# Output rows of a convolution and mixture kernel formed on TensorE, with a PSUM ring of three and two single banks

**Chip, cores, metric.** One core of one Trainium2 chip. The time is that of one execution on the device, in microseconds; the median of several executions is quoted with their spread. Engines are named as in the profile: PE (TensorE), PEld (its weight loads), DVE (VectorE), ACT (ScalarE), POOL (GpSimd), SP (SyncE).

## The reference

2048 tokens of 640 channels. A long convolution along the tokens makes the first residual; a router then picks 8 tokens for a gated feed-forward, whose result is added to those rows only. Cut to what the change touches:

```python
h = layernorm(x) * (1 + ca) + sa
x = x + ga * A(h, k, v, ...)             # conv by FFT, per channel
h = layernorm(x) * (1 + cb) + sb
# B: r = h @ w_r; idx = 8 largest r;  upd = h with  y(idx) added to 8 rows
x = x + gb * B(h, w_r, w_gate, w_up, w_down)
```

So each output row is x + gb * (layernorm(x) * (1 + cb) + sb), and 8 of the 2048 rows get a small addition afterwards.

## The kernel before

x lies in `xq`, 16 tiles of 128 tokens by 640. The steps run in a hand-written order; a star behind a step's name in that order puts its evacuation on DVE instead of ACT. Four PSUM tiles of two banks each serve everything:

```python
psum = ctx.enter_context(tc.tile_pool(name="psum", bufs=4, space=bass.MemoryType.PSUM))
```

The rows are made in three steps: the base x + gb*sb on PE (t_BS, and t_BL for the last 128 channels), the normalised row on ACT or DVE (t_N), and two DVE passes (t_F). The sums of squares for the layernorm run on ACT (t_S).

```python
    def t_BS():
        for j in range(8):
            # ... cut
            for i in range(2):
                nc.tensor.matmul(ps[:, i, :], lhsT=ident[:], rhs=gbs[:, 0:512], start=True, stop=False)
                nc.tensor.matmul(ps[:, i, :], lhsT=ident[:], rhs=xq[:, 2 * j + i, 0:512], start=False, stop=True)
            evac(h_["base", j // 4][:, 2 * j % 8:2 * j % 8 + 2, 0:512], ps[:])
            yield
    # ... cut
    def t_N():
        for m in range(M):
            if evac.vector:
                V.tensor_scalar(out=xn(m), in0=xq[:, m, :], scalar1=rs2[:, m:m + 1], scalar2=nm2[:, m:m + 1],
                                op0=ALU.mult, op1=ALU.add)
            else:
                nc.scalar.activation(out=xn(m), in_=xq[:, m, :], func=ACT.Identity, scale=rs2[:, m:m + 1],
                                     bias=nm2[:, m:m + 1])
            yield
    def t_F():
        for j in range(8):
            x2 = xq[:, 2 * j:2 * j + 2, :]
            V.tensor_tensor(out=x2, in0=xn(2 * j, 2).rearrange("p (m d) -> p m d", m=2),
                            in1=gbo[:, None, :].to_broadcast([P, 2, D]), op=ALU.mult)
            V.tensor_tensor(out=x2, in0=x2, in1=h_["base", j // 4][:, 2 * (j % 4):2 * (j % 4) + 2, :], op=ALU.add)
            # ... cut
```

## Time and profile before

| | |
|---|---|
| median of 3 runs | 186.74 us (184.03 to 187.41) |
| profiled span | 183.9 us, mean granted clock 0.919 |
| last attention block added | 147.0 |
| router score ready | 156.6 |
| last output row on DVE | 175.2 |
| small addition ready (delta) | 178.6 |

The lower four rows are landmarks, read from the order of time: the end of the instruction that writes the thing, counted from the start of the span. They cut the tail into stages. The chain of waits, followed back from the end, is spread over the engines:

```profile
DVE 27%; DMA 27%; PE 24%; ACT 12%; issue 6%; SPq 2%; POOLq 1%; POOL 0%; DVEq 0%; ACTq 0%
```

No engine holds the path alone. The totals, slices and windows stand in the prediction.

### The profile page before, as it was taken

How to read it: one execution, taken by the hardware profiler on the slowest of the kernel's cores; microseconds unless marked ns; L12 is line 12 of the kernel's file. 1: busy time of each engine (PE TensorE's matmuls, PEld its weight loads, DVE VectorE, ACT ScalarE, POOL GpSimd, SP SyncE). 2: the span in 40 equal slices, each digit the busy share in tenths (PEclk: the TensorE clock that was granted, in tenths of full speed). 3: DMA queues.
4: the chain of work that ended last, by engine and by line, in shares of the span. 5: the costliest groups of instructions: out<-in, count | busy, mean ns of one | idle time of the engine just before them, and what ended most of it. 6: DMA issues, size and time to landing. Idle time of an engine off the chain costs nothing.

```text
span 183.9 us, 4109 instructions
## 1 busy us (share of the span) xinstructions
PE 144.0 (78%) x1664; PEld 112.5 (61%) x1664; DVE 157.7 (86%) x283; ACT 136.2 (74%) x180; POOL 33.2 (18%) x81
## 2 busy tenths in 40 slices
PE   0669989985989999939999969999679578165850
PEld 0225979952768679837679759998577342024840
DVE  5869998988979899977599999989979996999930
ACT  4368789792897979775599979999448999996000
POOL 7997500005001022010010020020200102100003
PEclk9999999999999999995799999999999999955555
DMA  6999989999999999992041999994768099705540
GB/s 108 152 204 278 313 186 326 272 198 274 265 292 320 338 304 309 176 200 114 0 171 61 212 320 324 368 338 183 200 261 224 8 293 362 310 4 219 207 153 2
DMA packets 68668, 40.68 MB, mean 221 GB/s; under 512 B 44904, under 2 KB 64808, under 8 KB 68648
## 3 DMA queue, kind: packets, MB, share of 16 engines
q1 hardware_dynamic: 65160, 35.15, 72.7%
q0 software_dynamic: 1520, 5.25, 7.7%
q10 hardware_dynamic: 1968, 0.01, 0.7%
q8 instruction: 13, 0.21, 0.5%
q14 instruction: 7, 0.06, 0.1%
HBM read 24.67 MB, written 10.50 MB: 191 GB/s over the span
## 4 chain that ended last, share of the span: by engine, by line
DVE 27%; DMA 27%; PE 24%; ACT 12%; issue 6%; SPq 2%; POOLq 1%; POOL 0%; DVEq 0%; ACTq 0%
DMA kT<-in_A_k_dram 9%; PE ps L295 8%; ACT junk L404 7%; DMA kvd<-kvT 7%; DMA uA<-Ud 6%; DVE kvT L297 4%; DVE st L581 4%; PE ps L274 3%; PE ps L314 3%; DVE xq L641 3%; DMA Ud<-U 3%; DVE xq L643 3%; PE ps L384 2%; ACT U L58 2%; ACT A L58 2%
## 5 line engine op out<-in xcount | busy, mean ns | idle before, releaser
L58 ACT CAST A<-ps 128x1024 bf16<-128x1024 f32 x35 | 33.6, 1030 | 8.5 <-PE ps L274 8.5
L58 ACT CAST HX<-ps 128x1024 bf16<-128x1024 f32 x37 | 35.9, 1054 | 2.8 <-PE ps L318 2.8
L314 PE MATMUL ps<-A,FT 128*128 128x256 bf16 x160 | 36.2, 272 | 0.4 <-DVE kvT L297 0.4
L318 PE MATMUL ps<-A,FT 128*128 128x128 bf16 x160 | 35.0, 219 | 0.0
L316 PE MATMUL ps<-A,FT 128*128 128x128 bf16 x160 | 35.0, 219 | 0.0
L295 PE MATMUL ps<-kT,dg 128*128 128x512 bf16 x80 | 21.6, 426 | 7.0 <-DMA kT<-in_A_k_dram 7.0
L58 ACT CAST U<-ps 128x1024 bf16<-128x1024 f32 x20 | 19.8, 1048 | 5.0 <-PE ps L350 2.3
L295 PEld LDWEIGHTS <-dg 128*128 128x128 bf16 x80 | 8.5, 108 | 17.4 <-issue 3.8
L354 POOL DMA_DIRECT2D Ud<-U x10 | 5.7, 572 | 72.9 <-ACT U L58 62.9
L348 PE MATMUL ps<-IT,HX 128*128 128x256 bf16 x80 | 18.1, 273 | 0.8 <-DVE kvT L297 0.8
L350 PE MATMUL ps<-IT,HX 128*128 128x256 bf16 x80 | 18.1, 273 | 0.0
L297 DVE TENSOR_TENSOR kvT<-ps,vT 128x1024 bf16<-128x1024 f32 x10 | 12.1, 1220 | 6.9 <-PE ps L295 5.7
L318 PEld LDWEIGHTS <-FT 128*128 128x128 bf16 x160 | 15.7, 98 | 1.8
L316 PEld LDWEIGHTS <-FT 128*128 128x128 bf16 x160 | 15.6, 98 | 0.9 <-issue 0.8
L314 PEld LDWEIGHTS <-FT 128*128 128x128 bf16 x160 | 15.7, 98 | 0.3
L237 POOL TENSOR_SCALAR dg<-ident,shk_f 128x128 bf16<-128x128 bf16 x16 | 10.3, 659 | 20.0 <-PE ps L295 20.0
L384 PE MATMUL ps<-RAT,uA 128*128 128x128 bf16 x160 | 10.4, 219 | 4.2 <-DMA uA<-Ud 4.2
L404 ACT ACTIVATE junk<-xq 128x512 bf16<-128x512 bf16 (+1 forms) x23 | 12.2, 533 | 2.0 <-DVE xq L391 1.3
L389 DVE TENSOR_TENSOR t<-ps,h 128x1024 bf16<-128x1024 f32 x10 | 12.2, 1218 | 1.7 <-PE ps L384 1.6
L581 DVE BATCH_NORM_STATS2 st<-xq 128x6 f32<-128x320 bf16 x32 | 13.2, 478 | 0.5 <-DMA xq<-in_A_q_dram 0.5
L274 PE MATMUL ps<-RA,gA 128*128 128x256 bf16 x80 | 12.3, 309 | 1.5 <-DVE gA L281 1.5
L333 DVE TENSOR_TENSOR HX<-HX 128x2048 bf16<-128x2048 bf16 x10 | 12.2, 1225 | 0.4
(218 smaller groups left out, 308.6 us busy)
## 6 DMA issues: line engine op xcount, KB each, us to landing
Ud<-U POOLq DMA_DIRECT2D x10, 512.0 KB, 6.0
uA<-Ud SPq DMA_DIRECT2D x10, 512.0 KB, 6.5
early<-in_w_mod_dram SPq DMA_DIRECT2D x6, 800.0 KB, 7.3
gA<-in_A_ssm_k_dram SPq DMA_DIRECT2D x5, 512.0 KB, 5.0
kvd<-kvT SPq DMA_DIRECT2D x10, 256.0 KB, 3.9
xq<-in_A_q_dram SPq DMA_DIRECT2D x4, 640.0 KB, 6.4
xA<-kvd SPq DMA_DIRECT2D x5, 512.0 KB, 4.8
out_dram<-xq SPq DMA_DIRECT2D x4, 640.0 KB, 3.1
```

The source lines that it names most:

```text
L58: self.nc.scalar.copy(out=out, in_=in_)
L274: nc.tensor.matmul(ps[:, bb // 2, :, (bb % 2) * 8:(bb % 2) * 8 + 8], lhsT=src[:, 4 * g4 + bb, :], rhs=RA[:].rearrange("p k c e -> p (k c) ...
L295: nc.tensor.matmul(ps[:, i, :], lhsT=diags[b][:, j, :], rhs=kT[:, n0 - j:n0 - j + 512], start=(j == 0), stop=(j == 3))
L297: V.tensor_tensor(out=kvT[:, 1024 * i2:1024 * i2 + 1024], in0=ps[:].rearrange("p a b -> p (a b)"), in1=vT[:, 1024 * i2:1024 * i2 + 1024], ...
L314: nc.tensor.matmul(ps[:, i], lhsT=FT[:, 0, k2, :], rhs=A[:, 2 * k2:2 * k2 + 2, u, :], start=True, stop=False)
L316: nc.tensor.matmul(ps[:, i, 0, :], lhsT=FT[:, 1, k2, :], rhs=A[:, 2 * k2 + 1, u, :], start=False, stop=False)
L318: nc.tensor.matmul(ps[:, i, 1, :], lhsT=FT[:, 2, k2, :], rhs=A[:, 2 * k2, u, :], start=False, stop=True)
L348: nc.tensor.matmul(ps[:, i, :], lhsT=hx[:, k2, 0, 1, :], rhs=IT[:, k2, 1:3, :].rearrange("p a b -> p (a b)"), start=True, stop=False)
L350: nc.tensor.matmul(ps[:, i, :], lhsT=hx[:, k2, 1, 1, :], rhs=IT[:, k2, 0:2, :].rearrange("p a b -> p (a b)"), start=False, stop=True)
L384: nc.tensor.matmul(o, lhsT=uA[:, bb, cs * P:(cs + 1) * P], rhs=RAT[:, cs, :].rearrange("p (m e) -> p m e", e=8), start=(cs == 0), stop=(cs ...
L404: nc.scalar.activation(out=junk()[:, 0:n], in_=xq[:, m, b0 * P:b0 * P + n], func=ACT.Square, accum_out=dst[:, m:m + 1])
L581: V.bn_stats(out=st1[:, m, hf, :], in_=xq[:, m, hf * 320:hf * 320 + 320])
```

## The change

The intent is to take the output rows off DVE. The transposed tiles xT, which the router needs anyway, are kept; a row tile is xT times a diagonal matrix (five products of 128 x 128 x 128), plus two products whose operands have only 4 rows and which bring in mean, deviation and shift. DVE (or ACT, then DVE) scales the result and adds x. The squares become 32-column products on PE. PSUM becomes a ring of three double banks, one bank for small products and one for the squares. Some sums move to POOL, the square root gets two steps instead of three, a matrix of ones is written early, and the order is rewritten.

```diff
-    psum = ctx.enter_context(tc.tile_pool(name="psum", bufs=4, space=bass.MemoryType.PSUM))
+    psum = ctx.enter_context(tc.tile_pool(name="psum", bufs=1, space=bass.MemoryType.PSUM))
     def ps_tile(shape, dtype=F32):
-        return psum.tile(list(shape), dtype, name="ps", tag="ps")
+        return psum.tile(list(shape), dtype, name="ps", tag="ps", bufs=3)
+    def small_ps(shape, dtype=F32):
+        return psum.tile(list(shape), dtype, name="pq", tag="pq")
 ... (cut: t_BS, t_BL, t_N, t_S and the old t_F go)
+    def t_F():
+        for m in range(M):
+            ps = ps_tile([P, 1024])
+            for b in range(NB):
+                nc.tensor.matmul(ps[:, b * P:b * P + P], lhsT=xTs[b][:, m, :], rhs=dgb[:, b, :], start=(b % 4 == 0),
+                                 stop=False)
+            nc.tensor.matmul(ps[:, 0:512], lhsT=h_["rows"][:, m, :], rhs=st4[:, 0, 0:512], start=False, stop=True)
+            nc.tensor.matmul(ps[:, 512:D], lhsT=h_["rows"][:, m, :], rhs=st4[:, 0, 512:D], start=False, stop=True)
 ... (cut)
+            if evac.vector:
+                V.scalar_tensor_tensor(out=o, in0=ps[:, 0:D], scalar=rs2[:, m:m + 1], in1=xq[:, m, :], op0=ALU.mult,
+                                       op1=ALU.add)
+            else:
+                nc.scalar.mul(out=o, in_=ps[:, 0:D], mul=rs2[:, m:m + 1])
+                V.tensor_tensor(out=o, in0=o, in1=xq[:, m, :], op=ALU.add)
+    st4 = const.tile([4, 2, D], BF, name="st4")
+        h_["rows"] = ring.tile([4, M, P], BF, name="rows", tag="V")
+    def off():
+        return nc.gpsimd if evac.vector else V
-            V.tensor_tensor(out=Xr, in0=Xr, in1=T2[:, :, 1, :], op=ALU.subtract)
+            off().tensor_tensor(out=Xr, in0=Xr, in1=T2[:, :, 1, :], op=ALU.subtract)
 ... (cut: diagonal of the squares, shorter square root, token selection, a new order)
```

## The prediction

> **What bounds the kernel now.** I read the page's totals and forty slices first, then the busy time by windows, then the chain of waits and the order of time from 138 us on. Totals and slices:
>
> ```profile
> PE 144.0 (78%) x1664; PEld 112.5 (61%) x1664; DVE 157.7 (86%) x283; ACT 136.2 (74%) x180; POOL 33.2 (18%) x81
> ...
> DVE  5869998988979899977599999989979996999930
> ...
> PEclk9999999999999999995799999999999999955555
> DMA  6999989999999999992041999994768099705540
> ```
>
> DVE is the fullest engine: nines nearly everywhere except the start, slices 18 and 19, and the end. DMA is full up to slice 18 (about 83 us), then no longer. The windows (columns: busy PE, weight load, DVE, ACT, POOL, granted clock, DMA share, GB/s):
>
> ```profile
> 60.00:80.00 20.00, 19.50 (x201) 15.99 (x198) 18.56 (x40) 18.08 (x21) 1.93 (x3) 1.00 1.09 272
> 80.00:100.00 20.00, 17.20 (x128) 12.73 (x129) 15.80 (x32) 14.79 (x17) 1.64 (x5) 0.83 0.36 109
> 100.00:120.00 20.00, 18.02 (x224) 16.45 (x222) 19.69 (x23) 18.20 (x20) 1.43 (x3) 1.00 0.98 290
> ...
> 147.00:153.43 6.43, 5.03 (x48) 2.88 (x49) 5.16 (x20) 6.08 (x25) 0.25 (x2) 1.00 0.94 304
> 153.43:156.60 3.17, 2.01 (x9) 0.67 (x7) 2.65 (x16) 3.17 (x4) 0.86 (x3) 1.00 1.05 367
> 156.60:175.21 18.61, 9.66 (x230) 7.50 (x231) 17.92 (x41) 12.41 (x17) 0.95 (x2) 0.62 0.47 177
> ```
>
> From 100 to 120 us DVE is busy 19.69 of 20. From 80 to 100 something starves it: in order of time DVE waits 1.77 us for a product at 83.3 whose PE waited 2.87 us for a POOL memset of ones, and DVE then waits 2.01 us for a convolution queued behind. The last rows are the tail, cut at its landmarks: the last attention block is added at 147.0, the statistics end at 153.43, the router score r_bf is ready at 156.60, the last output row at 175.21. In that last window DVE is busy 17.92 of 18.61. The groups of the old tail:
>
> ```profile
> L643 DVE TENSOR_TENSOR xq<-xq,base 128x1280 bf16<-128x1280 bf16 x8 | 6.6, 825 | 0.3
> L641 DVE TENSOR_TENSOR xq<-FT,modv 128x1280 bf16<-128x1280 bf16 x4 | 3.3, 818 | 0.0
> L641 DVE TENSOR_TENSOR xq<-IT,modv 128x1280 bf16<-128x1280 bf16 x4 | 3.3, 816 | 0.0
> L404 ACT ACTIVATE junk<-xq 128x512 bf16<-128x512 bf16 x16 | 10.1, 630 | 1.8 <-DVE xq L391 1.3
> L653 DVE SCALAR_TENSOR_TENSOR tot<-ssq 128x16 f32<-128x16 f32 x1 | 0.2, 175 | 1.1 <-ACT junk L404 1.1
> ```
>
> The row to hold on to is the last: 12 us of squares on ACT delay DVE by only 1.1 us.
>
> **What the Trainium skill says.** (1) "GPSIMD Engine Reference", section 3.1: a two-input elementwise operation costs about 2.6 cycles an element. At its 1.2 GHz I estimate 1024 elements at 2.2 us plus the 0.21 us that a 128x16 sum takes here, so 2.4 us; no large POOL sum is in this trace. (2) "SBUF — State Buffer", "Who interferes with whom": a DVE instruction with two SBUF inputs, or in a two-port mode, shuts out a POOL instruction and the reverse; one with a PSUM and an SBUF input doesn't contend. The trace agrees in part: the 128x1024 table product took 1.63 us at 5.03 with POOL running and 1.22 us at 13.29 without. (3) "TensorE: Matmul & The Clock Gate", Part 1: the clock halves after some 3.4 us of idling. The trace agrees: 128x512 products start 0.216 us apart until 156, and 0.43 apart at 161, after a stretch with a handful of products. (4) "TensorEngine Tiling (Array Packing)", "Key Properties": changing the tiling mode drains the engine; no tiled product runs here.
>
> **The change part by part.** DVE, from measured rows.
> Removed: the two output passes, 8 x (0.82 + 0.825) = 13.2; 5 normalised rows, 2.0; 3 base copies at 1.21, 3.6; one IT copy, 1.2; two shorter square-root chains and their neighbours, about 0.8. Moved to POOL by the starred steps: 8 complex half-sums at 0.69 = 5.5, one h sum 1.5, one residual sum 0.7. Two evacuating products become ACT copy plus SBUF product: 2 x (1.22 - 0.69) = 1.1. Together 29.6.
> Added: 7 more PSUM casts in the middle (15 against 8) at 1.21 = 8.5. Output rows: seven fused at 128x640 from PSUM, which I interpolate from 195 ns at 48 and 1220 at 1024 elements as 0.82, and nine plain sums at 0.485 (the 128x640 row): 5.7 + 4.4 = 10.1. Diagonal of the squares, product and reduce over 512: 1.4. Token selection 1.4, rows copy 0.7, odd 0.2. Together 22.3. Net -7.3: 157.7 becomes 150.4.
> ACT: squares -12.1 (16 at the 0.755 spacing), 11 normalised rows -9.2, base -7.6, four casts fewer -4.2; IT +1.9, two copies +2.1, nine rows at about 0.75 +6.8, small +1.2. Net -21, so 115. It stops being anyone's rival.
> PE: base -9.4 (32 at 0.216, 8 at 0.3). Squares: 256 products of 32 columns at the 26 ns spacing that the 70 narrow products show (2.0 us), +6.7. Output rows at full clock: 5 x 0.056 + 0.216 + 0.056 = 0.55 a tile, +8.8 for 16. Transposed parts +0.9. Net +7.
> POOL: 8 x 2.4, one 2560-wide sum at some 5.8, one at 2.4, diagonals and vectors 6: about +34, so near 67 of 180.
>
> *Before the tail.* Up to the last block added, DVE sheds 5.5 + 1.5 + 0.7 + 1.1 on the moves, the three base copies (3.6) and the IT copy (1.2), and gains 8.5 in casts: -5. DVE there is busy 131 of 147 us, so I let the 5 through. The ones tile is now made at the start: the 80 to 100 window should lose about 2 more. The loads of k and v and the convolutions come earlier in the order, which fills the DMA hole of 80 to 100. Against it stand 1.5 us for a ring of three (PE can no longer fill two while DVE and ACT each drain one) and 2 us for POOL collisions. Sum -3.5.
>
> *The tail.* After the last block: 0.2 + 1.22 + statistics 2.4 + 0.2 + 1.22 + diagonal 1.4 + 0.2 = 6.8 on DVE, against 6.43. Taking the squares off ACT exposes only 1.1 us and the diagonal on DVE takes it back. Score chain: 12 short operations at 0.21, 2.5 against 3.17. Score to last row on DVE: three scalings 0.6, selection 2.1, rows copy 0.7, ranks 1.4, one-hot 0.44, token selection 2.0, rows 10.1 = 17.3, say 17.5 with gaps, against 18.61. Last row to scatter: up and down products are queued on PE behind all rows: 1.9 + 0.4 + 2.1 + 0.5 + 0.6 + 0.4 = 5.9 after the last row's products, which end 1.5 before the last sum: 4.4 against 3.69. Scatter 5.0 as before. Sum 36.2 against 36.9, -0.7.
>
> **Rivals.** *A, the whole reorder pays.* DVE totals say -7.3, and idle falls too because token selection no longer waits for normalised rows (3.1 us of PE waits on ACT in those products) and more work is fetched early. For it: everything removed sits on the fullest engine and ACT has 21 us to spare. It would make 174 to 177. *B, PE becomes the bound of the tail.* At half clock a row costs 5 x 0.107 + 0.43 + 0.107 = 1.07 us, 17 us for 16, as much as all DVE work there. For it: the stretch from the fourth transpose to the first row has some 5 us of thin PE work, and the clock stood at 0.62 there. Against it: rows keep PE busy and the clock should come back after three or four of them. It would give +3 to +5, 183 or so. *C, POOL collides.* Each moved 1024-wide sum holds POOL 2.4 us for 0.69 of DVE. If DVE stood behind half of 27 us, it would lose 13 and the kernel would be slower, 188. Against it: the starred steps stand ahead of row statistics (one SBUF input) and PSUM casts, which do not contend by (2). *D, DMA keeps the first 83 us.* Its share is full there and no byte goes away, so the middle's gain is only what follows: -2, giving 181.
>
> **Range and chances.** My step sums give -4.2 (182.5). I weight A more, as the starred order looks tuned to avoid collisions and the totals allow 7 to 10: 178.5 us, from 172.5 (A with the stall gone) to 184.5 (B or D). Faster means under 183.0. Chances: faster 0.75, same 0.20, slower 0.05. The three earlier runs spread from 184.03 to 187.41, which widens it.
>
> **What would show it.** Right: DVE total near 150, ACT near 115, POOL near 65; the last block added 3 to 5 us sooner; score to last row near 17.5; no wait for a memset of ones; clock back near 1 during the rows. Wrong: DVE sums with two SBUF inputs well over 0.69 beside POOL (C); row products 0.43 apart throughout (B); PE waiting on PSUM evacuation by several us more than before (the ring of three); the last block added at 147 as before (D).

## The result

The changed kernel takes 200.34 us (median of 4 runs, 199.34 to 200.76) against 186.46 (the three runs above and one more, 184.03 to 187.41). The ratio is 1.078, 95% interval 1.067 to 1.090: slower. (A ratio here is the mean time of one kernel's runs over that of the other's runs of the same rounds, so it is not quite the ratio of the medians. Executions over 1.5% slower than the fastest of the same kernel are left out of the means.) Landmarks:

| us | before | after | change of the stage | predicted |
|---|---|---|---|---|
| last attention block added | 147.0 | 149.7 | +2.7 | -3.5 |
| score ready | 156.6 | 158.8 | -0.5 | -0.3 |
| last output row | 175.2 | 189.3 | +11.9 | -1.1 |
| delta ready | 178.6 | 194.0 | +1.3 | +0.7 |
| end of span | 183.9 | 198.6 | -0.7 | 0 |

(The stage is the row's time less that of the row above it.) Most of the loss, 11.9 of 14.7 us, is in one stage, from the score to the last row. The page's totals and three of its forty-slice rows, after:

```profile
PE 162.9 (82%) x2006; PEld 123.5 (62%) x2010; DVE 156.0 (79%) x275; ACT 116.1 (58%) x137; POOL 67.8 (34%) x107
...
PE   0769999595999299999999999997795189799980
...
DVE  5879699987999966998899999999399866444430
...
PEclk9999999998899859999999999999699855555555
```

ACT and POOL came out as worked out (115 and 67). DVE shed 1.7 us rather than 7.3, and in the last eight slices it is no longer full: 6s and 4s where before had mostly 9s. PE is full there, and the clock row reads 5, half speed, for eight slices in a row. The windows of the tail, after (columns: length, then busy time of PE, PEld, DVE, ACT and POOL, granted clock, DMA share, GB/s):

```profile
149.74:158.80 9.06, 2.78 (x112) 2.33 (x112) 8.44 (x33) 2.81 (x14) 3.42 (x8) 0.91 0.75 253
158.80:189.32 30.52, 28.85 (x323) 16.79 (x324) 16.32 (x42) 8.55 (x13) 1.41 (x4) 0.50 0.21 76
189.32:198.60 9.28, 3.44 (x111) 3.03 (x108) 1.29 (x7) 0.00 (x0) 1.58 (x1) 0.50 0.13 38
```

The middle row answers to the last window in the prediction. DVE's work, 16.32 us, is close to what was worked out (17.3). But the stage lasts 30.52 us, because PE is busy for 28.85 of it, at a clock of 0.50. PE in order of time (start, duration, instruction; a trailing count joins equal ones):

```profile
161.79 0.71 PE L677 MATMUL ps<-dgb,xT 128*128 128x128 bf16 x5
162.43 0.60 PE L679 MATMUL ps<-st,rows 4*128 4x512 bf16 x1
162.83 0.31 PE L680 MATMUL ps<-st,rows 4*128 4x128 bf16 x1
163.07 0.71 PE L677 MATMUL ps<-dgb,xT 128*128 128x128 bf16 x5
```

Products overlap, so starts are what to subtract. A row takes 0.64 (five diagonal products) + 0.40 + 0.24 = 1.285 us, from 161.79 to 163.07. The prediction had 0.55. Sixteen rows at 1.285 are 20.6 us of PE, with token products between them. No gap is to be seen, and still the clock does not return. The chain of waits follows:

```profile
PE 43%; DVE 29%; DMA 15%; issue 5%; ACT 4%; POOLq 1%; POOL 0%; DVEq 0%; SPq 0%; ACTq 0%
```

PE has gone from 24% to 43%. That leaves two questions: why the clock stayed at half, and why the middle gained nothing.

For the second, busy time up to the last block, before and then after:

```profile
0.00:147.00 147.00, 124.73 (x1306) 99.35 (x1306) 130.79 (x204) 114.53 (x137) 29.62 (x74) 0.98 0.88 228
```

```profile
0.00:149.74 149.74, 127.86 (x1466) 101.40 (x1470) 129.94 (x195) 104.76 (x110) 61.38 (x95) 0.95 0.92 239
```

DVE's work there went from 130.79 to 129.94 us, 0.9 less instead of 5 less, and its idle time from 16.2 to 19.8. The casts of PSUM tiles are not what was misjudged: DVE has 13 casts of A at 1.22 us where it had 5, and 2 of HX where it had 3, so 15 against 8 as the prediction counted (the base's 3 went). What is missing is collision, in order of time on DVE and on POOL:

```profile
62.91 0.51 DVE L511 TENSOR_TENSOR modv<-modv 128x640 bf16<-128x640 bf16 x1
63.35 2.40 DVE L512 TENSOR_TENSOR modv<-modv 128x640 bf16<-128x640 bf16 x1
...
66.05 2.02 DVE L525 TENSOR_TENSOR modv<-modv 128x640 bf16<-128x640 bf16 x1
```

```profile
63.13 2.27 POOL L366 TENSOR_TENSOR HX<-HX,T 128x1024 bf16<-128x1024 bf16 x1
65.36 2.36 POOL L367 TENSOR_TENSOR HX<-HX,T 128x1024 bf16<-128x1024 bf16 x1
```

The same DVE sum takes 0.5 us alone and 2.40 when it meets a half-sum moved to POOL: it ends at 65.75, shortly after POOL's first sum does at 65.40. The two collisions cost 3.5 us of DVE time. Both are sums with both inputs in SBUF, the kind that the prediction's point (2) names (the page that it cites limits this to POOL instructions that read SBUF, as the half-sums do). The residual sums lost another 0.6 beside POOL (nine at 755 ns on average, against 692). That is nearly all of the missing 4.1. The longer idle time is mostly DVE waiting for PE: 4.5 us against 1.6 ahead of the products t, 2.1 against 0.3 ahead of casts of A; waits ahead of kvT fell from 5.7 to 4.6.

### The profile page after: what moved, and what is told of

Same layout as the page of the kernel before. It is cut to its first block, busy times and chain, and to the rows that moved or that the text cites. A ratio compares the mean times of both kernels' runs of the same rounds, so it can differ in the third digit from the quotient of the medians.

```text
span 198.6 us, 4788 instructions
## 1 busy us (share of the span) xinstructions
PE 162.9 (82%) x2006; PEld 123.5 (62%) x2010; DVE 156.0 (79%) x275; ACT 116.1 (58%) x137; POOL 67.8 (34%) x107
## 4 chain that ended last, share of the span: by engine, by line
PE 43%; DVE 29%; DMA 15%; issue 5%; ACT 4%; POOLq 1%; POOL 0%; DVEq 0%; SPq 0%; ACTq 0%
PE ps L325 7%; PE ps L344 5%; PE ps L677 5%; PE ps L679 4%; DMA early<-in_w_mod_dram 4%; PE ps L304 4%; DVE kvT L79 3%; DMA uA<-Ud 3%; DVE A L57 3%; ACT HX L59 3%; PE ps L499 3%; DMA kT<-in_A_k_dram 3%; PE ps L416 3%; DMA Ud<-U 3%; PE ps L348 3%
## 5 line engine op out<-in xcount | busy, mean ns | idle before, releaser
L59 ACT CAST HX<-ps 128x1024 bf16<-128x1024 f32 x38 | 36.7, 1024 | 3.8 <-PE ps L348 3.8
L344 PE MATMUL ps<-A,FT 128*128 128x256 bf16 x160 | 36.7, 275 | 0.5 <-DVE A L57 0.3
L59 ACT CAST A<-ps 128x1024 bf16<-128x1024 f32 x27 | 27.2, 1020 | 13.7 <-PE ps L304 10.7
L366 POOL TENSOR_TENSOR HX<-HX,T 128x1024 bf16<-128x1024 bf16 x4 | 8.6, 2159 | 31.4 <-DVE HX L364 31.4
L385 POOL DMA_DIRECT2D Ud<-U x8 | 4.7, 583 | 40.7 <-ACT U L59 40.7
L57 DVE CAST A<-ps 128x1024 bf16<-128x1024 f32 x13 | 15.5, 1220 | 2.2 <-PE ps L304 2.1
L79 DVE TENSOR_TENSOR kvT<-ps,vT 128x1024 bf16<-128x1024 f32 x9 | 10.9, 1219 | 4.6 <-PE ps L325 4.6
L79 DVE TENSOR_TENSOR t<-ps,h 128x1024 bf16<-128x1024 f32 x9 | 10.9, 1221 | 4.5 <-PE ps L416 4.5
L499 PE MATMUL ps<-early 128*128 128x320 bf16 x60 | 10.3, 325 | 4.7 <-DMA early<-in_w_mod_dram 2.4
L416 PE MATMUL ps<-RAT,uA 128*128 128x128 bf16 x160 | 11.5, 234 | 2.5 <-DMA uA<-Ud 2.4
```

Of the source, the lines that this page charges most:

```text
L57: self.nc.vector.tensor_copy(out=out, in_=in_)
L59: self.nc.scalar.copy(out=out, in_=in_)
L79: V.tensor_tensor(out=out, in0=acc, in1=other, op=ALU.mult)
L344: nc.tensor.matmul(ps[:, i], lhsT=FT[:, 0, k2, :], rhs=A[:, 2 * k2:2 * k2 + 2, u, :], start=True, stop=False)
L416: nc.tensor.matmul(o, lhsT=uA[:, bb, cs * P:(cs + 1) * P], rhs=RAT[:, cs, :].rearrange("p (m e) -> p m e", e=8), start=(cs == 0), stop=(cs ...
L499: nc.tensor.matmul(ps[:, hf, 0:320], lhsT=silu_bc[:, t, :], rhs=wms[a][:, t, hf * 320:hf * 320 + 320], start=(t == 0), stop=(t == NB - 1))
```

## The experiments

Sixteen kernels ran, in four groups; the kernel before ran beside each. In every group several runs of the kernel before counted as slow, and its median moved between 185.85 and 187.67, so ratios within some 1.5% are mostly not resolved. The profiled runs of e_mix and b_rows2 counted as slow as well; their landmarks are given with that reserve. A landmark comes from one profile: the nine kernels whose steps are the same up to the last block put it at 148.3 to 149.8, so a difference of about a microsecond there says little. All sixteen passed the comparison with the reference.

**The theory: the granted clock.** The rows' products are too thin for the clock to return, so PE runs them at half speed. *Rival 1:* it is only a cold start, and busy products would have kept a clock that was already up. *Rival 2:* PE's added work is too long in itself. *Rival 3:* POOL's collisions or the ring of three cost most of the 14 us.

### e_warm: dummy products ahead of the rows

```diff
+    def t_WU():
+        for n in (14, 3, 3):         # after the last sums; before the parts; before the ranks
+            pw = psum.tile([P, 512], F32, name="pw", tag="pg")
+            for _ in range(n):
+                nc.tensor.matmul(pw[:], lhsT=ident[:], rhs=xTs[0][:, 0:4, :]..., start=True, stop=True)
+            yield
```

> The changed kernel, with 20 dummy products of 128x512 (14 behind the last router product, 3 before the statistics are transposed, 3 before the ranks) into a free bank, so that TensorE does not idle from 155 to 162 us. Theory 'cold start' (the gap halves the clock and the row products never get it back, but would keep it): clock near 1.0 through the rows, 0.55 to 0.65 us a row instead of 1.29, about 188 us. Theory 'low activity' (the row products themselves, half of whose time feeds only 4 of 128 rows of the array, are too thin to hold the clock): the clock is full for the first 3 to 7 us of rows, then falls to 0.5 again, 194 to 198 us.

196.65 us (1 run). The clock by windows of 5 us, columns as above:

```profile
160.00:165.00 5.00, 5.00 (x52) 2.71 (x49) 3.89 (x13) 2.62 (x5) 0.95 (x2) 1.00 0.02 3
165.00:170.00 5.00, 3.94 (x71) 2.75 (x69) 3.87 (x9) 2.34 (x3) 0.00 (x0) 0.78 0.53 197
170.00:175.00 5.00, 5.00 (x57) 2.81 (x56) 2.12 (x8) 0.80 (x1) 0.00 (x0) 0.50 0.15 53
```

The first rows run at full clock, 0.76 us apart (starts at 161.68, 162.44, 163.19). After 5.5 us of such rows come the token products, 8 columns wide, and within 0.8 us of their start the clock falls; from 170 to the end it stays at 0.50, with rows 1.285 apart and PE busy 5.00 of 5. This run doesn't tell whether the rows or the token products lost the clock; e_swap below does. The warm start gains 3.7 us of the loss. Even at full clock a row is 0.76 and not 0.55.

### e_pad: the 4-row operands filled with zeros to 128 rows

```diff
-    st4 = const.tile([4, 2, D], BF, name="st4")
+    st4 = const.tile([P, 2, D], BF, name="st4")            # rows 4 to 127 set to zero by POOL
-        h_["rows"] = ring.tile([4, M, P], BF, name="rows", tag="V")
+        h_["rows"] = ring.tile([P, M, P], BF, name="rows", tag="V")   # same
```

> The changed kernel, with the four-row operands of the two added products of a row (moving 4x640, stationary 4x128) padded with zeros to 128 rows; same results, no product more. Theory 'low activity': the clock comes back to 1.0 within 3 to 7 us of rows, then 0.6 us a row, about 190 us. Theory 'cold start alone': as the changed kernel, 1.2 to 1.3 us a row, 200 us. If only the change of the array's tiling between 4-row and 128-row products costs, the row falls from 1.29 to about 1.07 at clock 0.5 and the time to 196.

191.58 us (1 run), 8.8 us less, for the same products. PE in order of time:

```profile
162.27 0.74 PE L682 MATMUL ps<-dgb,xT 128*128 128x128 bf16 x5
162.81 0.63 PE L684 MATMUL ps<-st,rows 128*128 128x512 bf16 x1
163.23 0.31 PE L685 MATMUL ps<-st,rows 128*128 128x128 bf16 x1
163.34 0.57 PE L682 MATMUL ps<-dgb,xT 128*128 128x128 bf16 x5
163.74 0.38 PE L684 MATMUL ps<-st,rows 128*128 128x512 bf16 x1
...
165.66 0.44 PE L682 MATMUL ps<-dgb,xT 128*128 128x128 bf16 x5
...
166.21 0.28 PE L682 MATMUL ps<-dgb,xT 128*128 128x128 bf16 x2
```

In the third row the products get shorter in mid-row (0.63, then 0.38): the clock is back, as the prediction had it, after two and a half rows. From there a row is 0.55 us (165.66 to 166.21). The padding also removes 0.21 us a row at full clock (0.76 against 0.55) and 0.22 to 0.24 at half (1.285 against 1.05): two changes between 128-row and 4-row products. After the token products three rows run at half clock, and then it returns again. Rows of zeros do no arithmetic that matters, and they bring the clock back: this is the direct evidence for the theory.

### e_norows: the two 4-row products left out

```diff
-            nc.tensor.matmul(ps[:, 0:512], lhsT=h_["rows"][:, m, :], rhs=st4[:, 0, 0:512], start=False, stop=True)
-            nc.tensor.matmul(ps[:, 512:D], lhsT=h_["rows"][:, m, :], rhs=st4[:, 0, 512:D], start=False, stop=True)
```

> The changed kernel without the two four-row products of each output row (result wrong on purpose: the mean and shift terms are missing), so that only full 128x128 products are left in a row. Theory 'low activity': clock back near 1.0, TensorE no longer the bound, rows at the pace of DVE and ACT (0.65 us), about 188 us. Theory 'cold start': the clock stays at 0.5, a row costs 5 x 0.107 to 0.128 = 0.55 to 0.64 us on TensorE, again about 188 us; the granted clock tells the two apart, not the time.

188.89 us (1 run); the rows are incomplete (the missing terms are small). The clock is between 0.62 and 0.72 in the windows from 160 to 180, with gaps on PE, and the last row comes at 178.4. These are averages of full and half: by windows of a microsecond the clock is 1.00 from 163 to 166 and again from 174 to 176, and 0.50 from 167 to 173, after token products. So it does come back for full-height (128-row) products, but it is not held near 1.0, as the theory had it. So with the two thin products go 11.5 of the 13.9 us: their own time, and part of what the low clock took from everything else. Against rival 2, that PE's added work is too long in itself, e_pad is the cleaner witness, as it has all the products and loses 8.8 us; but the next runs show that something of rival 2 is left.

### e_nopool and b_ring3: rival 3

```diff
     def off():
-        return nc.gpsimd if evac.vector else V
+        return V
```

> The changed kernel with its ten starred sums put back from POOL to DVE (the moved half-sums, the wide sum and the residual sum), nothing else. Theory 'POOL collisions cost' (DVE products of 128x640 beside POOL took 2.40 and 2.02 us instead of 0.48, some 3.5 us in all): DVE busy rises by the 7.7 us of the moved work less these 3.5 or more, and the time stays within 2 us of 200 or falls. Theory 'moving them pays': 203 to 206.

200.78 us (198.91 to 202.15), ratio to before 1.081 (1.050 to 1.111): no different from the changed kernel. The 128x640 sums are back at 0.48 us, and in exchange DVE has its half-sums again; the last block is added at 150.0, against 149.7. The moves took some 7.7 us of work off DVE (the prediction's figure), but up to the block its busy time is only 2.7 less with them (129.94 against 132.65), and the block comes only 0.3 us sooner, which single profiles can't resolve.

```diff
-    psum = ctx.enter_context(tc.tile_pool(name="psum", bufs=4, space=bass.MemoryType.PSUM))
+    psum = ctx.enter_context(tc.tile_pool(name="psum", bufs=3, space=bass.MemoryType.PSUM))
```

> The kernel before with its PSUM ring cut from four pairs of banks to three, nothing else (two banks lie idle). If the ring of three is what puts the last attention block 2.7 us later in the changed kernel, this costs 2 to 4 us (188 to 190). If the ring is nearly free, under 1 us.

This is the kernel before with a ring of three: 187.70 us (187.16 to 187.93), ratio 1.016 (1.003 to 1.029). The last block comes at 148.8 instead of 147.0. By this profile the ring costs 1.8 us in the middle; neither part of rival 3 explains 14.

### e_padwarm: both remedies

Padding as in e_pad and dummies as in e_warm.

> Padding and the 20 dummy products together in the changed kernel. In the padded run alone the clock stood at 0.5 for the first two and a half rows (160 to 163 us) and again for three rows after the narrow token products. If both the gap before the rows and the narrow products cool the clock, the dummies mend the first only: 1 to 2 us better than padding alone, about 190. If the clock is lost again whatever is done, no gain: 191 to 192.

189.46 us (187.84 to 191.07), ratio 1.023 (0.989 to 1.057). The clock is 1.00 from 155 to 165, 0.97 to 170, 0.69 from 170 to 175 (the token products again) and 0.99 to 180. Yet from the score at 157.8 to the last row at 179.3 it is still 21.5 us, against 18.6 before. PE in order of time shows where some of it goes:

```profile
165.04 1.35 PE L784 MATMUL pq<-T,xq 128*128 128x8 bf16 x48
167.72 0.40 PE L787 MATMUL pq<-sel,onesf 128*128 128x16 f32 x2 [1.33 <-DVE sel L780]
168.05 0.18 PE L789 MATMUL pq<-cinfo,ohC 128*40 128x3 bf16 x1
168.16 0.96 PE L784 MATMUL pq<-T,xq 128*128 128x8 bf16 x32
168.98 0.44 PE L689 MATMUL ps<-dgb,xT 128*128 128x128 bf16 x5
```

PE works in program order. The token products stand ahead of the next row, and in their midst PE waits 1.33 us for a sum that DVE does behind other rows: no row starts between 164.49 and 168.98.

### e_mix: token products between the rows

```diff
+        (the two DVE operations that make sel2 move up one step)
             for m in range(M):
                 nc.tensor.matmul(pxs[:, b, :], lhsT=xq[:, m, b * P:(b + 1) * P], rhs=onehot[:, m, :], ...)
+            if b < NB - 1:
+                yield
-F:2 T F F* F:2 T F* F F* F:2 T F* F F*:2 T:4
+F:2 T F F* F T F T F* T F T F* T F:2 T F* F F*:2 T:4
```

> The changed kernel with padded rows and dummy products, and two more edits against what is left of the loss in the row stage: the sums over the chosen tokens are issued one step earlier, so that TensorE does not stand 1.3 us behind them, and the narrow token products go out block by block with a row between each, so that they leave no long stretch of little work in which the clock falls. Theory (the clock fell at 170 because of the narrow stretch, and rows then waited): granted clock above 0.95 throughout 158 to 178, last row 2 to 3 us earlier than the 179.3 of the padded and warmed kernel, 186.5 to 187.5 us. Rival (VectorE's own work of 16.3 us and the chain of the choice bound the stage): last row stays within 1 us of 179.3, 188.5 to 190 us.

187.98 us (186.22 to 189.50), ratio 1.011 (0.996 to 1.027). The clock is now 1.00 from 160 to 175: the thin products, spread among rows, no longer pull it down. But the last row comes at 178.8, only 0.5 us sooner, and the stage is 20.8 us: the rival of this run was right. The fourteen dummies here delayed the choice by 1.2 us, as PE was not done with them when the score came, and the next thin stretch (70 gate products at 172.6) lowered the clock for the last rows.

### m_tail, b_rows, b_rows2: only the rows, in the order of before

m_tail puts the order of before in front of the change's own tail (padded, dummies, ring of three). b_rows keeps also the ring of four and the squares on ACT, so that only the rows move (with the early ones and the short root).

```diff
 (b_rows)
-    ps = psum.tile(..., tag="ps", bufs=3);  small products in tag="pq"
+    ps = psum.tile(..., tag="ps", bufs=4);  small products in the same ring
-    t_GR (squares on PE)
+    t_S  (squares on ACT, as before), order of before up to the rows
```

> The order of work of the kernel before up to the attention blocks, with everything else of the change (ring of three, squares on TensorE, rows on TensorE), padded and with dummies. Tells the new order of the middle from the rest. If the new order is what puts the last attention block at 149.7 us instead of 147.0, the block comes at 147 to 148 here and the run ends at 185 to 187. If the ring of three is all of it (the ring alone moved it to 148.8), the block stays at 149 to 150 and the run ends near 189.

> The order of the kernel before and its ring of four pairs, squares on ACT as before, and only the rows formed on TensorE (padded, with the dummies); no base, no normalised rows. The part 'rows on TensorE' alone, with the clock held up. If the gain that I expected of this part (about 1 us) is real once the clock is there, 184 to 186 against 186. If rows on TensorE lose even so (the clock falls after the narrow products, the router products queue behind rows), 188 to 192.

m_tail took 200.63 us (1 run) and b_rows 193.47 (192.69 to 194.49), ratio 1.050 (1.031 to 1.069). Both are spoiled by a fault of mine, in b_rows at

```profile
137.19 1.89 PE L415 MATMUL ps<-RAT,uA 128*128 128x128 bf16 x16 [7.11 <-DMA uA<-Ud]
```

The change writes the last block's results from SyncE's queue, where before used POOL's. In the spliced order those writes waited 13.4 us for ACT, and the loads behind them in the same queue, which PE needed, waited with them. In m_tail PE waits 6.42 us for the same load; I take it to be the same fault, but did not mend that one. The mended b_rows:

```diff
-                    (nc.sync if b == NB - 1 else nc.gpsimd).dma_start(out=Ud[...], in_=U[:])
+                    nc.gpsimd.dma_start(out=Ud[...], in_=U[:])
 (and the row stage of e_mix)
```

> The earlier trial of rows on TensorE in the order of before, mended: all attention results are written to memory from GpSimd's queue as before (in the earlier trial the last block's writes stood ahead of the loads in SyncE's queue and held TensorE 7.1 us), and the row stage has the interleaved order. PSUM ring of four pairs, squares on ScalarE, padded rows, dummies. If the loss before the rows is the order and the ring: last attention block at 146 to 148, r_bf at 156 to 157, last row at 174.5 to 177, 181 to 184.5 us, faster than before. Rival (another part of the change is guilty, or the row stage stays over 20 us): 186 to 190 us.

187.64 us (185.29 to 190.09), ratio 1.005 (0.986 to 1.024): as before, within what can be resolved. The last block comes at 148.4, the score at 157.0, the last row at 177.2, 20.2 us later (a slow run). The clock is 0.97 to 1.00 from 155 to 170, then 0.73 and 0.84. So with full-height products, a clock mostly held up and the order of before in the middle, the move of the rows to PE is not shown to pay: a gain or a loss under some 2% can't be told apart here.

### e_pad64, e_w64, e_swap: what the clock listens to

Padding to 64 rows in place of 128:

```diff
-    st4 = const.tile([P, 2, D], BF, name="st4")
+    st4 = const.tile([64, 2, D], BF, name="st4")           # and rows likewise
```

> The changed kernel with the 4-row operands padded with zeros to 64 rows only. If the clock follows the share of the array's rows in use: half of the array, so the clock comes back later or in part, rows between 0.8 and 1.2 us apart, 192 to 197 us. If what counts is whether a product spans the whole array (no change of tile size between products): as in the changed kernel, clock near 0.50 from 160 on, rows about 1.28 apart, 197 to 200 us. If four rows were below some small threshold and any fuller product does: as padded to 128, rows 0.55 apart, 190 to 192 us.

199.03 us (1 run), clock 0.50 in every window from 155 to 185, rows 1.29 us apart. Half the array is as bad as 4 rows. Two things go with both: less of the array in use, and changes of size between products. The next two runs part them; both are the changed kernel, unpadded.

```diff
 (e_w64, ahead of the choice)
+        for _ in range(28):
+            nc.tensor.matmul(pw[:], lhsT=ident[0:64, :], rhs=X4[0:64], start=True, stop=True)
 (e_swap, same place)
+        for _ in range(24):
+            nc.tensor.matmul(pw[:], lhsT=ident[:], rhs=X4, start=True, stop=True)
+            nc.tensor.matmul(pw[:, 0:16], lhsT=ident[0:4, :], rhs=X4[0:4, 0:16], start=True, stop=True)
```

> The changed kernel (4-row operands, nothing padded) with 28 dummy products of 64 rows by 512 columns, all of one size and without a gap, issued after the last block's sums and before the choice. If filling the array is what raises the clock: 0.50 throughout, 0.43 us apart, the dummies take 12 us and the kernel is some 6 to 8 us longer than 200.3. If the change of tile size is what held the clock down in the rows: the clock comes to 1.00 after about 4 us as with whole-array dummies, and the later dummies are 0.22 us apart.

206.31 us (1 run). The 28 products begin at 155.33 and follow one another without a gap, all of one size. Windows:

```profile
155.00:156.00 1.00, 0.96 (x16) 0.59 (x13) 0.96 (x3) 0.00 (x0) 0.00 (x0) 1.00 1.12 371
156.00:157.00 1.00, 1.00 (x6) 0.45 (x5) 0.86 (x6) 0.00 (x0) 0.72 (x3) 1.00 0.26 76
157.00:158.00 1.00, 1.00 (x4) 0.34 (x3) 0.83 (x6) 0.00 (x0) 0.64 (x4) 0.67 0.08 26
...
160.00:165.00 5.00, 5.00 (x13) 1.63 (x11) 0.00 (x0) 0.00 (x0) 0.00 (x0) 0.50 0.01 3
```

The clock was up when they began, and fell under them, with PE busy 1.00 of 1. The two microseconds before them were thin too (PE busy 0.16 and 0.26 of 1), which may have helped it to fall; but 7 us more of them did not bring it back, where in e_warm 14 full-height products did so in 3.7 us. So products that use half the array's rows do not win the clock, and no change of size is involved.

> The changed kernel with 24 pairs of dummies at the same place: a whole-array product of 512 columns and a 4-row product of 16 columns after each, so that the tile size changes twice per pair while nearly all the work fills the array. If filling counts: clock 1.00 after 4 to 5 us, pairs then some 0.35 us apart (0.22 plus the switch and the small product). If the change of tile size keeps the clock down: 0.50 throughout, pairs about 0.6 to 0.7 us apart.

209.78 us (1 run). PE in order of time, then a window in the midst of the pairs and two after them:

```profile
160.09 0.61 PE L661 MATMUL pw<-xT,ident 128*128 128x512 bf16 x1
160.62 0.19 PE L662 MATMUL pw<-xT,ident 4*128 4x16 bf16 x1
160.75 0.61 PE L661 MATMUL pw<-xT,ident 128*128 128x512 bf16 x1
```

```profile
160.00:165.00 5.00, 5.00 (x17) 1.56 (x16) 0.00 (x0) 0.00 (x0) 0.00 (x0) 0.50 0.01 3
...
173.00:174.00 1.00, 1.00 (x13) 0.52 (x11) 0.54 (x3) 0.58 (x2) 0.33 (x1) 1.00 0.00 0
...
175.00:176.00 1.00, 1.00 (x9) 0.53 (x8) 1.00 (x3) 1.00 (x2) 0.10 (x1) 0.75 0.00 0
```

For 15.7 us whole-array products of 512 columns alternate with tiny 4-row ones, and the clock stays at 0.50. When the pairs end (170.6) it comes up within 1.5 us, in which PE did little but the 16 transposes of the row parts, 128 rows in and 4 columns out. So size changes alone hold it down too.

The last window settles rival 1. The change's own rows begin at 172.84, at full clock, and from 175.5 on the clock is at 0.50 (0.75 on average in that window), with PE busy throughout and before any of the 8-column token products. Thin rows alone lose a clock that was up.

By their own expectations e_w64 spoke for filling the array and e_swap for changes of size. One reading made after the runs covers both: what counts is the share of the time in which the array's rows are in use, not whether PE is busy. (Rows and not columns, since the 4-column transposes brought the clock back.) With 0.43 us for 512 columns at half clock (from the trace of before), I estimate that share as 0.43/0.66 = 65% for e_swap (the rest of a pair goes into the two changes), (0.53 + 0.27)/1.29 = 62% for e_pad64, 50% for e_w64, and (0.53 + 0.02)/1.285 = 43% for the changed kernel; full for e_pad. The first four stay at or fall to 0.50, and the last returns to 1.00. Two runs fit only with additions. By the same working the rows of e_warm used (5 x 0.056 + 0.01)/0.755 = 38% and still ran at 1.00 for 5.5 us, so the share would have to be averaged over several microseconds; and e_mix, with 0.55 us of row in every 0.95, used about 60% and kept 1.00 from 166 to 171, so less would have to suffice to hold the clock than to win it. That a share is what the chip measures is inferred, not shown, and where the limits lie stays open.

### e_ring4: the change's own order with the ring of four

```diff
 (e_mix with)
-    ring of three, squares as products on PE
+    ring of four, squares on ACT behind the last attention block
```

> The changed kernel's own order of the middle, with the ring of four pairs in place of three and two single banks, squares on ScalarE as before, padded rows, dummies, interleaved row stage: differs from e_mix (187.98 us, r_bf at 158.0) mainly by the ring and the squares. If the ring of three is what ate the gain of the middle: last attention block at 143.5 to 145.5, r_bf at 154.5 to 156, 183.5 to 186 us. If the order itself did: r_bf stays at 157 to 159 and the time at 187 to 189.5 us.

194.85 us (194.35 to 195.65), ratio 1.050 (1.040 to 1.059). The total says nothing about the ring: with the squares on ACT after the last block, the score waits for them until 162.5, a flaw of this splice. The last block alone can be read: 146.9, against 148.3 to 149.8 in the nine kernels of the same order with the ring of three. But the squares on PE, 192 products before the block, are gone here too, so this run does not part the ring from the squares; b_ring3 (148.8 against 147.0, one profile each) is the only run of the ring alone.

### b_ones and b_ones2: the part that might be worth keeping

```diff
 (b_ones: the kernel before with)
-        onesf = early[:, 9728:9984].bitcast(F32)
-        nc.gpsimd.memset(onesf, 1.0)
+    onesf = const.tile([P, P], F32, name="onesf")          # written by POOL early on
 (b_ones2: also the two-step square root)
```

> The kernel before with one piece of the change alone: the matrix of ones is written on GpSimd early in the program, where before it is written on the way to the small sums. The prediction gave this -2 us. If the wait was on the path of the middle: 184 to 185.5 us against 186.5 (ratio 0.987 to 0.995), last attention block at 145 to 146.5 (147.0 before). Rival: another wait takes its place (attention tiles, DMA) and the time stays within 0.5 us.

> Before, with the early matrix of ones and the shorter reciprocal square root of the change (two steps in place of three), nothing else. The two keep what the change gained without its rows: 183 to 185 us against about 186.4, ratio 0.983 to 0.995; rival: within noise, ratio 0.995 to 1.005.

b_ones: 184.23 us (183.77 to 186.37), ratio 0.998 (0.983 to 1.013). b_ones2: 186.51 (184.95 to 187.49, 6 runs), ratio 1.004 (0.997 to 1.012). In single profiles the last block came at 143.5 and 145.0, sooner than the 147.0 of before, but the times do not confirm a gain: the larger trial leaves no room for one of over half a per cent. No version of these sixteen is shown to beat the kernel before.

## Why the prediction was wrong

The prediction was 178.5 us and faster; it was 200.34 and slower. By its own steps:

- **Output rows on PE, "5 x 0.056 + 0.216 + 0.056 = 0.55 a tile": the failed step.** The figure is right for full-height products at full clock (e_pad: 0.55). In the changed kernel a row took 1.285: 1.05 from half the clock, the rest from two changes of size. 16 x (1.285 - 0.55) = 11.8 us on PE, where DVE's own 16.3 us no longer covers it.
- **Rival B was the right one, and was dismissed by a false sentence:** "rows keep PE busy and the clock should come back after three or four of them". They did keep PE busy, 28.85 of 30.52 us, and the clock did not come back. The page that the prediction named, "TensorE: Matmul & The Clock Gate" of the Trainium skill, says in Part 1 that idling halves the clock and activity restores it; the prediction took any busy product for activity. With zeros in the other 124 rows it came back after two and a half. The size that B was given, 1.07 a row, lacked the changes of size; and "+3 to +5" took it for work beside DVE's, where PE's token products queue in the same order as the rows. Its point (4) says that no tiled product runs in the trace of before; the records show a few with 16 rows (16*128, at 158.74), and it did not ask what the change's 4-row products would cost.
- **Score to last row, 17.5:** the 17.3 of DVE work (16.3 measured) was about right and no longer mattered. Even with the clock mostly held the stage is 20.2 to 21.5. Why is shown only in part: rows wait in PE's queue behind the token products, but e_mix, which removed one such wait, gained 0.5.
- **Before the tail, -3.5; measured +2.7.** "Ring of three +1.5" has 1.8 in b_ring3. "POOL collisions 2": about 4 of DVE time. "-5 from DVE's moves": the moves and casts came as counted, and with the collisions DVE's work up to the block fell by 0.9 only. "-2 for the ones": the block came earlier by 2.0 and 3.5 in two profiles, not confirmed in time. What the sum lacked is that DVE's idle time rose by 3.6, mostly in waits for PE. How that divides between the order, the ring and the convolutions' loads was not settled.
- **Statistics to the score -0.3, last row to scatter 4.4, scatter 5.0:** measured -0.5, 4.7 and 4.6, with the cut at delta, about 0.3 before the prediction's.
- **Totals:** ACT 115 (116.1) and POOL 67 (67.8) right; DVE 150.4 (156.0), of which the collisions are about 4; PE +7 (+18.9), of which the rows' 11.8. The squares were put too high: 64 of their products take 0.66 us, some 10 ns each, not 26. For POOL, "GPSIMD Engine Reference" of the Trainium skill, section 3.1, held: about 2.6 cycles an element give an estimate of 2.2 us for 1024 elements, and a sum alone took 2.12; the start-up of 0.21 that the prediction added was not needed.
- **Rivals A and D:** neither has PE as the bound of the tail. C happened on a small scale: about 4 us of DVE time, not 13.

The weight given to A ("the starred order looks tuned") was a guess over a sum, and the page had warned: the clock row of before already ended in 5s.

## What to carry to other kernels

Before moving work to TensorE where it has little to do, ask for each product how many of the array's 128 rows it uses, and price it at half clock unless full-height products fill most of the stretch (an estimated 65% was not enough in e_swap); zeros up to 128 rows can be cheaper than 4 rows. Work added to an engine that runs in order also delays whatever short chain shares its queue. And a sum of costs says nothing until each term is put on the engine that will bound the stage after the change.

## What the Trainium skill lacked or had wrong

- "TensorE: Matmul & The Clock Gate" of the Trainium skill, Part 1, describes the clock by how busy the engine has been, and its table "Why this matters for your kernels" advises to keep TensorE busy for 4 us. Here it was busy 28.85 of 30.52 us at 0.50. What is lacking is the height of the products: 64-row ones, back to back for 10 us, let the clock fall from 1.00 to 0.50 within 3 us and did not bring it back (e_w64), and 128-row ones did (e_pad).
- The same page has nothing on changes of size: pairs of a 128-row and a 4-row product held the clock at 0.50 for 15.7 us without a gap.
- "TensorEngine Tiling (Array Packing)", "Key Properties", says that a change of mode drains the engine, with no figure: two changes a row cost 0.21 us at full clock (0.76 against 0.55) and 0.22 to 0.24 at half (1.285 against 1.05).
- "TensorE: Matmul & The Clock Gate", Part 1, says that starts are never less than about 25 ns apart. That is too general: the 8-column products of the feed-forward kept to it (70 in 1.90 us, 27 ns each, in e_pad), but the 32-column products of the squares, on four column positions, ran 64 in 0.66 us, 10 ns each. The same page's Part 3 lets products on different tiles overlap; what Part 1 lacks is this exception.
